# GpSimd takes the negative logits of q from the shifted ones, and the low parts of the MLP weights move behind q's logits on VectorE

## The chip, the cores and the metric

One core of one Trainium2 chip runs the whole kernel as one launch. The metric is the time of the launch in microseconds (us), as the device counts it; the median of repeated runs is given. Smaller is better. The engines are named as the profile names them: PE (TensorE, matrix products), PEld (its weight loads), DVE (VectorE), ACT (ScalarE), POOL (GpSimd) and SP (SyncE, which issues most DMAs).

## What is computed

The input x has 2048 tokens of 512 channels. First comes a linear attention with 32 heads of 16 channels, then an MLP across the tokens, each behind a layer norm and with a residual:

```
q, k, v = split(layernorm(x) @ wqkv)
pq = q @ w_phi (per head);  pk likewise
phi_q = concat(softmax(pq), softmax(-pq));  phi_k likewise
num = phi_q @ (phi_k^T v);  den = phi_q . sum(phi_k) + 1e-6
h  = x + (num / den) @ wo
h2 = h + (gelu(layernorm(layernorm(h))^T @ w1 + b1) @ w2 + b2)^T
```

What matters here is the pair of softmaxes per head of 16 channels: for the first the logits are shifted by their maximum (v - max), for the second the negated logits are shifted by the minimum (min - v). Both halves then go through one exponential.

## The kernel before, in words

**Tiles.** The 2048 tokens are cut into 16 tiles of 128. Every large product is made in three passes from operands that are split into a high and a low part: the high part is a rounded copy made on ACT, the low part is the difference (source minus high part), made on DVE or POOL. `mm3` (L60) issues the three matmuls, so L62, L63 and L64 stand for most of PE's work before the last stage.

**Stages.** (1) The projections of k and v with their softmax and sums, together with the q projections of tiles 0 to 5; (2) a ramp, L420 to L508, that ends k and v, sums k's features over all tiles (`zacc`, finished on DVE in L480 and spread by a product with ones in L487) and starts q's tiles 6 to 9; (3) the loop of L630, one iteration `it` per tile, which makes the attention's output and the residual and fills the first two pairs of MLP columns; (4) the rest of the MLP's first product, then its second product (L761), to the end.

**Order.** From L419 to L669 the order of the instructions on PE, DVE, ACT and POOL is the order of the program text: each engine takes its instructions one after the other, and one that waits holds up all behind it. SP's order, and the order after L669, is set by the planner.

**q's logits.** `logit_ops` (L137) returns three steps for one tile of q, whose projection lies in PSUM (`pu`): the maximum over each head (`mx`, L152), the minimum (`mn`, L153), and `shift`, which writes v - max into the first half of `eq` (L145). For tiles 6 to 15 (`pool` is true), `shift` also has ACT copy the raw logits from PSUM into the second half of `eq` (L147), and `negate` (L156), which is called later, has POOL turn that half into min - v (L160). For other tiles DVE makes both halves (L150). The exponential is L171. The PSUM tile is free for the next product once its last reader is done: DVE's L145 and ACT's L147.

**One iteration of the loop,** for the parts that matter here. PE: `s_num` (L543, the attention's numerator of tile it-1 into the PSUM tile `tn`), `s_wo` (tile it-2 times wo, into `po`), `s_tr` (transposes of tile `it` into `tn`, L525), a q projection (into `pu`), and `fill` products of the MLP (into `pu` too, L62 to L64 with `hs` and `whi`/`wlo`). `tn` has one buffer, so the transposes of a tile wait until ACT's `oh` (L547) and DVE's `ol` (L552) have read the numerator of the tile before. ACT: `pht` (L527), the exponential, the raw copy (L147), `hn` and `hs` (L584, L57), high parts of MLP weights (`whi`, L604), then in the next iteration `oh`. POOL: `s_pq` (L460), `s_rstd` (L579, L580), `s_ez` (L442), `negate` (L160), the low part of `hs` (L58). DVE: the list `ops` of L652, in which the steps of `ol`, of q's logits and of q's sums (L216) take turns with the six steps of `s_den` (L451 to L457); into it go `s_h` (L568, the residual) and `flush` (L593), which makes the low parts of the weights (`wlo`, L596) whose high parts are there.

Iterations 0 to 5 have logits of q in this list; from iteration 6 on there are none left.

Of the kernel before, what the change touches and what calls it, by code (L numbers as in the profile page):

```python
# [11 lines left out]
AF = mybir.ActivationFunctionType  # L12
# [5 lines left out]
P = 128  # L18
S, D, H, DH, F = 2048, 512, 32, 16, 1792
NT = S // P  # L20
# [3 lines left out]
NPR = 2 * NG  # L24
# [9 lines left out]
def block_kernel(ctx: ExitStack, tc: tile.TileContext, x, xT, wT, phic, wo, w1, b1, w2, b2,  # L34
                 kvmask, ident_in, out):
    nc = tc.nc
# [95 lines left out]
    MN = []  # L132

    def signs(e):
        return e.rearrange("p g (a c h d) -> p (g a) c h d", a=2, c=2, h=2)

    def logit_ops(src, e, pool):  # L137

        v = src.rearrange("p (j h d) -> p j h d", h=2, d=DH)
        ev = signs(e)  # L140
        mx = wk.tile([P, NPR, 2], F32, name="mx")
        mn = wk.tile([P, NPR, 2], F32, name="mn")

        def shift():
            nc.vector.tensor_sub(ev[:, :, 0], v, mx.unsqueeze(3).to_broadcast([P, NPR, 2, DH]))  # L145
            if pool:
                nc.scalar.activation(ev[:, :, 1], v, AF.Copy)  # L147
                MN.append((ev, mn))
            else:
                nc.vector.tensor_sub(ev[:, :, 1], mn.unsqueeze(3).to_broadcast([P, NPR, 2, DH]), v)  # L150

        return [lambda: nc.vector.tensor_reduce(mx, v, axis=AX.X, op=ALU.max),  # L152
                lambda: nc.vector.tensor_reduce(mn, v, axis=AX.X, op=ALU.min),  # L153
                shift]

    def negate():  # L156

        if MN:
            ev, mn = MN.pop(0)
            nc.gpsimd.tensor_sub(ev[:, :, 1], mn.unsqueeze(3).to_broadcast([P, NPR, 2, DH]), ev[:, :, 1])  # L160

    def turns(*lists):

        return [ops[i] for i in range(max(map(len, lists))) for ops in lists if i < len(ops)]

    def run(*lists):
        for op in turns(*lists):
            op()
# [42 lines left out]
    def q_sum(t):  # L211

        assert t < SUMS or t - SUMS in W, "a tile's sums would go where others are still wanted"
        SQ[t] = sums[:, t % SUMS]
        e = signs(EQ[t])
        return [lambda c=c: nc.vector.reduce_sum(SQ[t][:, :, 1 - c], e[:, :, c], axis=AX.X) for c in range(2)]  # L216
# [144 lines left out]
    def q_mm():  # L361
        if q["mm"] < NT:
            PS[q["mm"]] = proj(q["mm"], wqh, wql, ps_q, "pu")
            q["mm"] += 1

    def q_logits(lag):
        n = q["logits"]
        if n < min(NT, q["mm"] - lag + NT * (q["mm"] == NT)):
            EQ[n] = big.tile([P, NG, P], F32, name="eq", tag="big")
            q["logits"] += 1  # L370
            return logit_ops(PS[n], EQ[n], n >= len(Q_AT))
        return []
# [7 lines left out]
    def q_sums(lag):  # L380
        n = q["sum"]
        if n < min(NT, q["exp"] - lag + NT * (q["exp"] == NT)):
            q["sum"] += 1
            return q_sum(n)
        return []
# [10 lines left out]
    v = 2  # L396
# [62 lines left out]
    def s_pq(t):  # L459
        nc.gpsimd.tensor_mul(heads(EQ[t]), heads(EQ[t]), W[t].rearrange("p g c h -> p (g c h)").unsqueeze(2).to_broadcast([P, 2 * H, DH]))  # L460

    def lead(it, mm):

        if 0 <= it + 3 < NT:
            s_ez(it + 3)
        negate()
        for _ in range(mm):
            q_mm()
        q_exp(0)
# [51 lines left out]
    def s_tr(t):  # L521
        PHT[t] = ak.tile([P, NG, P], F32, name="pht")
        ptr = ps_t.tile([P, 2, 4, P], F32, name="tn")
        for g in range(NG):
            nc.tensor.transpose(ptr[:, g // 4, g % 4, :], EQ[t][:, g, :], ident)  # L525
        for half in range(2):
            nc.scalar.activation(PHT[t][:, half * 4:half * 4 + 4, :], ptr[:, half], AF.Copy)  # L527

    def s_kv():

        pt = ps_o.tile([P, 2, P], F32, name="po")
        for b in range(2):
            nc.tensor.transpose(pt[:, b, :], kvS[:, 2 * b:2 * b + 2, :].rearrange("p n f -> p (n f)"), ident)
        nc.scalar.activation(kvB, pt, AF.Copy)

    def s_num(t):

        pn = ps_t.tile([P, 2, 4, P], F32, name="tn")[:, :, 0:2]
        for b in range(2):
            for c in range(4):  # L540
                for r in range(2):
                    rows, cols = slice(64 * r, 64 * r + 64), slice(32 * c, 32 * c + 32)
                    nc.tensor.matmul(pn[cols, r, b, :], kvB[rows, b, cols], PHT[t][rows, 4 * b + c, :],  # L543
                                     start=True, stop=True, skip_group_check=True)
        oh = ak.tile([P, 2, 2, P], F32R, name="oh")
        ol = ak.tile([P, 2, 2, P], F32R, name="ol")
        nc.scalar.activation(oh, pn, AF.Copy)  # L547
        OS[t] = oh, ol, pn

    def s_ol(t):  # L550
        oh, ol, pn = OS[t]
        return [lambda: nc.vector.tensor_sub(ol, pn, oh)]  # L552

    def s_wo(t):
        oh, ol, _ = OS.pop(t)
        PO[t] = po = ps_o.tile([P, D], F32, name="po")
        for j in range(4):
            mm3(po, oh[:, j // 2, j % 2, :], ol[:, j // 2, j % 2, :], woh[:, j, :], wol[:, j, :], j == 0, j == 3)

    def s_x(t):  # L560
        HT[t] = ak.tile([P, D], F32, name="h", bufs=4)
        nc.sync.dma_start(HT[t], x[t * P:(t + 1) * P, :])

    def s_h(t):

        h = HT[t]
        VE[t] = ak.tile([P, 4], F32, name="ve2", bufs=3)
        nc.vector.scalar_tensor_tensor(h, PO.pop(t), 1.0, h, op0=ALU.mult, op1=ALU.add, accum_out=VE[t][:, 2:3])  # L568
        nc.sync.dma_start(out[t * P:(t + 1) * P, :], h)

    def s_moments(t):

        junk = ak.tile([P, D], F32, name="hj", bufs=1)
        nc.scalar.activation(VE[t][:, 1:2], VE[t][:, 2:3], AF.Copy, scale=-1.0 / D)
        nc.scalar.activation(junk, HT[t], AF.Square, bias=VE[t][:, 1:2], accum_out=VE[t][:, 3:4])
        nc.scalar.activation(VE[t][:, 0:1], VE[t][:, 3:4], AF.Identity, scale=(1.0 + EPS) / D, bias=eps2)

    def s_rstd(t):
        nc.gpsimd.tensor_tensor(r2[:, t:t + 1], VE[t][:, 0:1], mhalf[:, :1], op=ALU.pow)  # L579
        nc.gpsimd.tensor_mul(VE[t][:, 1:2], VE[t][:, 1:2], r2[:, t:t + 1])  # L580

    def s_hn(t):
        hn = ak.tile([P, D], F32, name="hn")
        nc.scalar.activation(hn, HT[t], AF.Identity, scale=r2[:, t:t + 1], bias=VE[t][:, 1:2])  # L584
        HN[t] = big.tile([P, 2, D], F32R, name="hs", tag="big")
        split(HN[t][:, 0], HN[t][:, 1], hn, nc.gpsimd)
# [29 lines left out]
    def fill(p, pool=None):  # L616

        t = FN[p]
        FN[p] = t + 1
        if FL[p] <= t:  # L620
            fill_load(p)
            flush()
        if t == 0:
            PU[p] = [pool.tile([P, D], F32, name="pu", tag="pu") for _ in range(2)]
        a, b = WI[p, t - t % 2]
        for c in range(2):
            mm3(PU[p][c], a[:, t % 2, c * P:(c + 1) * P], b[:, t % 2, c * P:(c + 1) * P],
                HN[t][:, 0], HN[t][:, 1], t == 0, t == NT - 1)

    for it in range(NT + 3):  # L630
        if 0 <= it < NT:
            s_x(it)
        if 0 <= it - 1 < NT:
            s_num(it - 1)
        if 0 <= it - 3 < NT:
            s_moments(it - 3)
        if 0 <= it - 2 < NT:
            s_wo(it - 2)
        if it == 1:
            run(q_logits(0))  # L640
            q_mm()
        if 0 <= it < NT:
            s_tr(it)
        if it == 0:
            s_kv()
        if 0 <= it + 1 < NT:
            s_pq(it + 1)
        if 0 <= it - 3 < NT:
            s_rstd(it - 3)
        lead(it, 1)  # L650
        den = s_den(it + 2) if it + 2 < NT else []
        ops = turns((s_ol(it - 1) if 0 <= it - 1 < NT else []) + q_logits(1) + (q_sums(0) if it > 0 else []), den)  # L652

        ops[3:3] = ([lambda: s_h(it - 2)] if 0 <= it - 2 < NT else []) + [flush]
        run(ops)
        if it > 0:
            negate()
        if 0 <= it - 3 < NT:
            s_hn(it - 3)
        if FN[0] <= it - LAG:  # L660
            fill(0, ps_f)
        for _ in range(2):
            if q["logits"] == NT and FN[1] <= it - LAG:
                fill(1, ps_q)
        for p in range(2):
            if it >= LAG - 2 and FL[p] <= FN[p] + 1:
                fill_load(p)
# [199 lines left out]
```

## Time and profile before

| What | Value |
|---|---|
| median of 3 runs | 534.8 us (534.78 to 535.04) |
| profiled execution, its own time | 535.27 us |
| its span, first to last instruction | 533.5 us |
| mean granted TensorE clock | 0.999 |
| PE, DVE, ACT, POOL busy | 98%, 72%, 52%, 43% of the span |

The span of the profiled execution is shorter than its time by 1.77 us, which lie before the first and behind the last instruction. PE is busy for nearly all of the span, so what counts is where PE waits: a view of waits lists who waited for whom, and a timeline of one engine gives for each instruction its start, its duration, its line, output and inputs, and in square brackets the idle time before it with what ended it. Matmuls overlap, so that on PE the distance from start to start tells more than the duration.

### The profile page before, as it was taken

The page shows a single profiled execution, that of the slowest core. Times are in us where ns is not written, and L with a number is a line of the kernel's source. Part 1 is how long each engine was busy: PE and PEld are TensorE (multiplying, and loading weights), DVE is VectorE, ACT ScalarE, POOL GpSimd, SP SyncE. Part 2 cuts the span into 40 slices and gives each one's busy share as a digit, 9 for nine tenths or more (in the row PEclk, how much of TensorE's full clock was granted, in tenths as well). Part 3 has the DMA queues.
Part 4 walks back from the last instruction along what each step waited for, and adds up shares of the span by engine and source line. Part 5 has one row for each costly group of instructions (what it writes and reads, how often), then busy time and mean ns, then how long its engine had stood idle before and what let it go on. Part 6 is the DMA issues. An engine that isn't in the chain of part 4 may idle for free.

```text
span 533.5 us, 9887 instructions
## 1 busy us (share of the span) xinstructions
PE 523.4 (98%) x3872; PEld 451.0 (85%) x3872; DVE 382.5 (72%) x680; ACT 277.6 (52%) x470; POOL 228.3 (43%) x180
## 2 busy tenths in 40 slices
PE   8999999999999899999999999999999999999995
PEld 7888888887877777778788888888899999999995
DVE  6893999878798979784235523835768878887784
ACT  6998833525447777666766423525443343343340
POOL 2589699877876978985345000000001101100110
PEclk9999999999999999999999999999999999999999
DMA  8544310022302223333355333533014556535631
GB/s 303 196 124 119 86 35 21 1 62 78 101 1 83 95 81 119 120 109 111 95 159 182 99 100 99 159 111 87 20 41 110 138 149 146 131 120 120 158 78 43
DMA packets 45487, 55.85 MB, mean 105 GB/s; under 512 B 3968, under 2 KB 33024, under 8 KB 45440
## 3 DMA queue, kind: packets, MB, share of 16 engines
q1 hardware_dynamic: 43136, 51.38, 30.3%
q0 software_dynamic: 2016, 3.67, 5.1%
q8 instruction: 30, 0.49, 0.4%
q10 hardware_dynamic: 288, 0.17, 0.1%
q14 instruction: 17, 0.14, 0.1%
HBM read 46.81 MB, written 8.39 MB: 103 GB/s over the span
## 4 chain that ended last, share of the span: by engine, by line
PE 90%; DVE 5%; ACT 3%; issue 1%; POOL 1%; DVEq 0%; ACTq 0%; POOLq 0%
PE py L761 26%; PE pu L62 12%; PE pu L64 12%; PE pu L63 11%; PE po L62 3%; PE pv L63 2%; PE tn L525 2%; PE pv L64 2%; PE pv L62 2%; PE pk_ps L62 2%; PE po L63 2%; PE po L64 2%; PE pk_ps L64 2%; PE pk_ps L63 2%; PE tn L543 2%; PE kvp L207 1%
## 5 line engine op out<-in xcount | busy, mean ns | idle before, releaser
L799 POOL DMA_DIRECT2D out<-ot x14 | 12.5, 1001 | 212.1 <-DVE ot L797 212.1
L761 PE MATMUL py<-uf,whi 128*128 128x256 f32 x560 | 96.2, 283 | 0.0
L62 PE MATMUL pu<-hs,whi 128*128 128x512 f32 x224 | 87.6, 394 | 0.7 <-ACT eq L147 0.7
L57 ACT ACTIVATE whi<-wraw 128x1792 fp32r<-128x1792 f32 x28 | 47.7, 1705 | 77.9 <-PE py L761 62.9
L63 PE MATMUL pu<-hs,whi 128*128 128x512 f32 x224 | 87.2, 389 | 0.0
L64 PE MATMUL pu<-hs,wlo 128*128 128x512 f32 x224 | 87.0, 390 | 0.2 <-DVE wlo L596 0.2
L761 PEld LDWEIGHTS py<-uf,whi 128*128 128x128 f32 x560 | 83.3, 192 | 0.0
L596 DVE TENSOR_TENSOR wlo<-wraw,whi 128x512 fp32r<-128x512 f32 x56 | 46.3, 841 | 45.2 <-ACT whi L604 44.0
L761 PE MATMUL py<-uf,wlo 128*128 128x256 f32 x280 | 69.9, 283 | 0.0
L58 DVE TENSOR_TENSOR wlo<-wraw,whi 128x1792 fp32r<-128x1792 f32 x28 | 56.6, 2023 | 17.8 <-ACT whi L57 17.8
L604 ACT ACTIVATE whi<-wraw 128x512 fp32r<-128x512 f32 x56 | 34.4, 627 | 45.6 <-PE pu L63 41.6
L62 PEld LDWEIGHTS pu<-hs,whi 128*128 128x128 f32 x224 | 42.1, 188 | 9.3 <-ACT eq L147 1.2
L64 PEld LDWEIGHTS pu<-hs,wlo 128*128 128x128 f32 x224 | 42.1, 188 | 9.3 <-DVE wlo L596 0.6
L761 PEld LDWEIGHTS py<-uf,wlo 128*128 128x128 f32 x280 | 49.7, 192 | 0.0
L63 PEld LDWEIGHTS pu<-hs,whi 128*128 128x128 f32 x224 | 42.1, 188 | 8.4
L442 POOL TENSOR_TENSOR ez<-eq,zB 128x1024 f32<-128x1024 f32 x16 | 39.5, 2474 | 0.1
L761 PE MATMUL py<-un,whi 128*128 128x256 f32 x224 | 38.4, 283 | 0.0
L195 POOL TENSOR_TENSOR pk<-pk,sk 128x1024 f32<-128x1024 f32 x16 | 31.1, 1944 | 9.8 <-DVE sk L194 9.0
L460 POOL TENSOR_TENSOR eq<-eq,w 128x1024 f32<-128x1024 f32 x16 | 31.0, 1940 | 5.9 <-DVE w L457 5.9
L527 ACT ACTIVATE pht<-tn 128x512 f32<-128x512 f32 x32 | 17.4, 596 | 30.8 <-PE tn L525 30.8
L761 PEld LDWEIGHTS py<-un,whi 128*128 128x128 f32 x224 | 33.2, 192 | 0.1
L199 POOL TENSOR_TENSOR zacc<-zacc,pk 128x1024 f32<-128x1024 f32 x13 | 31.3, 2406 | 0.6
(165 smaller groups left out, 1192.8 us busy)
## 6 DMA issues: line engine op xcount, KB each, us to landing
wraw<-in_w SPq DMA_DIRECT2D x112, 256.0 KB, 2.9
xraw<-in_xT SPq DMA_DIRECT2D x16, 256.0 KB, 3.1
xh<-in_x SPq DMA_DIRECT2D x16, 256.0 KB, 2.6
h<-in_x SPq DMA_DIRECT2D x16, 256.0 KB, 3.1
out<-h SPq DMA_DIRECT2D x16, 256.0 KB, 2.0
out<-ot POOLq DMA_DIRECT2D x14, 256.0 KB, 4.6
wraw<-in_wT SPq DMA_DIRECT2D x12, 256.0 KB, 5.0
wo<-in_wo SPq DMA_DIRECT2D x4, 256.0 KB, 4.7
```

Of the source, the lines that this page charges most:

```text
L57: nc.scalar.activation(hi, src, AF.Copy)
L58: lo_engine.tensor_sub(lo, src, hi)
L62: nc.tensor.matmul(o, ah, bh, start=first, stop=False)
L63: nc.tensor.matmul(o, ah, bl, start=False, stop=False)
L64: nc.tensor.matmul(o, al, bh, start=False, stop=last)
L195: nc.gpsimd.tensor_mul(heads(PK[t]), heads(PK[t]), sk.unsqueeze(2).to_broadcast([P, 2 * H, DH]))
L199: nc.gpsimd.tensor_add(zacc, zacc, PK[t])
L442: nc.gpsimd.tensor_mul(EZ[t], EQ[t], zB)
L460: nc.gpsimd.tensor_mul(heads(EQ[t]), heads(EQ[t]), W[t].rearrange("p g c h -> p (g c h)").unsqueeze(2).to_broadcast([P, 2 * H, DH]))
L596: LO.append(nc.vector.tensor_sub(wl_, raw, wh_).ins)
L604: nc.scalar.activation(wh_, raw, AF.Copy)
L761: nc.tensor.matmul(o, a[x], b[:, y], start=start and i == 0, stop=stop and i == 2, skip_group_check=True)
```

## The change

For tiles 6 to 15, ACT's raw copy is gone. `negate` on POOL first makes min - max (an operation on 128x32 elements, written over `mn`), then subtracts the shifted logits from it: (min - max) - (v - max) = min - v. The list `MN` carries `mx` too. In the loop, `flush` is no longer put next to `s_h` but at place 7 of the list where there are logits of q, that is behind `shift`; where there are none it stays where it was.

```diff
         def shift():
             nc.vector.tensor_sub(ev[:, :, 0], v, mx.unsqueeze(3).to_broadcast([P, NPR, 2, DH]))
             if pool:
-                nc.scalar.activation(ev[:, :, 1], v, AF.Copy)
-                MN.append((ev, mn))
+                MN.append((ev, mx, mn))
...
         if MN:
-            ev, mn = MN.pop(0)
-            nc.gpsimd.tensor_sub(ev[:, :, 1], mn.unsqueeze(3).to_broadcast([P, NPR, 2, DH]), ev[:, :, 1])
+            ev, mx, mn = MN.pop(0)
+            nc.gpsimd.tensor_sub(mn, mn, mx)
+            nc.gpsimd.tensor_sub(ev[:, :, 1], mn.unsqueeze(3).to_broadcast([P, NPR, 2, DH]), ev[:, :, 0])
...
-        ops = turns((s_ol(it - 1) if 0 <= it - 1 < NT else []) + q_logits(1) + (q_sums(0) if it > 0 else []), den)
-
-        ops[3:3] = ([lambda: s_h(it - 2)] if 0 <= it - 2 < NT else []) + [flush]
+        ql = q_logits(1)
+        ops = turns((s_ol(it - 1) if 0 <= it - 1 < NT else []) + ql + (q_sums(0) if it > 0 else []), den)
+
+        at = 7 if ql else 3
+        ops[at:at] = [flush]
+        ops[3:3] = [lambda: s_h(it - 2)] if 0 <= it - 2 < NT else []
         run(ops)
```

In iterations 2 to 5 DVE's order was `ol`, L451, `mx`, `s_h`, `flush`, L452, `mn`, L454, `shift`, L455, sum, L456, sum, L457. It is now `ol`, L451, `mx`, `s_h`, L452, `mn`, L454, `shift`, `flush`, L455, sum, L456, sum, L457.

## The prediction

> **What bounds the kernel now.** I read the page's busy times first, then the list of what PE waited for, then the timelines of the engines around each of those waits.
>
> ```profile
> span 533.5 us, 9887 instructions
> ...
> PE 523.4 (98%) x3872; PEld 451.0 (85%) x3872; DVE 382.5 (72%) x680; ACT 277.6 (52%) x470; POOL 228.3 (43%) x180
> ```
> ```profile
> PE tn L525 <- POOL hs L58: 1.4, 1, 1.4
> ...
> PE pu L62 <- ACT eq L147: 0.7, 1, 0.7
> PE pk_ps L487 <- DVE zacc L480: 0.5, 1, 0.5
> PE pu L64 <- DVE wlo L596: 0.2, 1, 0.2
> ```
>
> PE is busy for all but 10.1 us. A change on other engines can only win where PE waits, and these are the only waits of PE behind the start-up. Two lie close to what is changed: the transposes of tile 4 (1.4 us) and a fill product that waits for the raw copy itself (0.7 us). The chain that ended last is PE alone from 386.98 to 525.23:
>
> ```profile
> 386.98 138.25 PE py L761 x1152
> ```
>
> So what PE gains or loses before reaches the end in full, as long as no other engine falls behind. Now the two waits, on PE (start, duration):
>
> ```profile
> 165.25 0.39 PE L64 MATMUL po<-woh,ol 128*128 128x512 f32 x1
> 165.48 1.03 PE L525 MATMUL tn<-ident,eq 128*128 128x128 f32 x8
> ...
> 169.18 0.67 PE L543 MATMUL tn<-pht,kvB 64*32 64x128 f32 x32
> ...
> 172.41 0.39 PE L64 MATMUL po<-woh,ol 128*128 128x512 f32 x1
> 174.16 1.06 PE L525 MATMUL tn<-ident,eq 128*128 128x128 f32 x8 [1.37 <-POOL hs L58]
> ...
> 185.43 0.39 PE L64 MATMUL pu<-hs,wlo 128*128 128x512 f32 x1
> 186.55 0.50 PE L62 MATMUL pu<-hs,whi 128*128 128x512 f32 x1 [0.74 <-ACT eq L147]
> ```
>
> Unhindered, the transposes start 0.23 after the last `po` product (165.25 to 165.48). Tile 4's should start at 172.64 and start at 174.16: **1.52 us** lost. The fill product should start at 185.66 and starts at 186.55: **0.89 us**.
>
> What held tile 4? `tn` has one buffer, read by ACT's `oh` and then by DVE's `ol`:
>
> ```profile
> 167.53 1.15 ACT L171 ACTIVATE eq<-eq,r 128x1024 f32<-128x1024 f32 x1
> 170.85 0.60 ACT L147 ACTIVATE eq<-pu 128x512 f32<-128x512 f32 x1 [2.17 <-DVE eq L145]
> 171.34 0.81 ACT L584 ACTIVATE hn<-h,ve,r 128x512 f32<-128x512 f32 x1
> 172.18 0.63 ACT L57 ACTIVATE hs<-hn 128x512 fp32r<-128x512 f32 x1
> 172.72 0.58 ACT L547 ACTIVATE oh<-tn 128x512 fp32r<-128x512 f32 x1
> ```
> ```profile
> 165.97 0.68 DVE L568 SCALAR_TENSOR_TENSOR h<-po,h 128x512 f32<-128x512 f32 x1
> 166.57 2.81 DVE L596 TENSOR_TENSOR wlo<-wraw,whi 128x512 fp32r<-128x512 f32 x2
> 169.41 0.68 DVE L153 TENSOR_REDUCE mn<-pu 128x32 f32<-128x512 f32 x1
> 170.14 0.68 DVE L145 TENSOR_TENSOR eq<-pu,mx 128x512 f32<-128x512 f32 x1
> 172.38 0.22 DVE L457 TENSOR_TENSOR w<-smq,den 128x64 f32<-128x64 f32 x1
> 173.33 0.69 DVE L552 TENSOR_TENSOR ol<-tn,oh 128x512 fp32r<-128x512 f32 x1 [0.73 <-ACT oh L547]
> ```
> ```profile
> 165.06 0.55 POOL L579 TENSOR_TENSOR r<-ve,mhalf 128x1 f32<-128x1 f32 x1
> 165.69 0.19 POOL L580 TENSOR_TENSOR ve<-ve,r 128x1 f32<-128x1 f32 x1
> 165.84 2.39 POOL L442 TENSOR_TENSOR ez<-eq,zB 128x1024 f32<-128x1024 f32 x1
> 171.52 1.07 POOL L160 TENSOR_TENSOR eq<-mn,eq 128x512 f32<-128x512 f32 x1 [3.29 <-ACT eq L147]
> 172.89 1.27 POOL L58 TENSOR_TENSOR hs<-hn,hs 128x512 fp32r<-128x512 f32 x1 [0.30 <-ACT hs L57]
> ```
>
> The numerator was done at 169.85, but ACT sat idle for 2.17 us until 170.85 for DVE's `shift`, made the raw copy, `hn` and `hs`, and reached `oh` at 172.72. `ol` ended at 174.02, and PE went on at 174.16. (The list names POOL's `hs`, which ended at the same moment. The transposes read neither `hs` nor `hn`, so I take `ol`.) DVE was late because its two `wlo` took 2.81 us, ahead of `mn` and `shift`.
>
> **The port.** Why 2.81? A `wlo` alone took 0.69:
>
> ```profile
> 183.75 0.69 DVE L596 TENSOR_TENSOR wlo<-wraw,whi 128x512 fp32r<-128x512 f32 x1
> ```
>
> POOL's `ez` ended at 168.23; two uncovered operations at the pitch of 0.6 then end at 169.4, which is when the two did (166.57 + 2.81 = 169.38). So the first stood still until `ez` was through. The ramp shows who goes next when both wait:
>
> ```profile
> 125.05 1.29 DVE L480 TENSOR_TENSOR zacc<-zacc,pk 128x512 f32<-128x512 f32 x2 [0.41 <-POOL pk L195]
> ...
> 127.47 1.55 DVE L431 TENSOR_TENSOR wol<-wo,woh 128x512 fp32r<-128x512 f32 x1
> ```
> ```profile
> 123.08 1.94 POOL L195 TENSOR_TENSOR pk<-pk,sk 128x1024 f32<-128x1024 f32 x1 [1.09 <-DVE sk L194]
> 127.07 1.40 POOL L160 TENSOR_TENSOR eq<-mn,eq 128x512 f32<-128x512 f32 x1 [2.05 <-ACT eq L147]
> ```
>
> POOL's `negate` took 1.40 instead of its usual 1.06 (it waited some 0.34 for DVE's running `wol`) and ended at 128.47; the `wol` issued at 127.47 ended at 129.02, 0.55 after it. So they take turns, one instruction each, and the loser waits for the whole one. The operations that collide have both inputs in SBUF (`wlo`, `wol`, `zacc`; all of POOL's here).
>
> **The change part by part.**
>
> ```profile
> L147 ACT ACTIVATE eq<-pu x10: 577/598/601, 126.4 to 185.9; 128x512 f32<-128x512 f32 x10
> L160 POOL TENSOR_TENSOR eq<-mn,eq x10: 1060/1064/1402, 127.1 to 186.8; 128x512 f32<-128x512 f32 x10
> ```
>
> *Removed:* ten ACT copies of 0.598, 6.0 us of ACT. As PE is the bound, only their place counts: ACT no longer waits there for `shift`, and a `pu` buffer is free after `shift`. *Added:* ten POOL operations of 128x32. The trace has none of that size. Bounds: 0.19 (L580, 128x1) and 1.06 (128x512); on the line between them 32 columns give 0.19 + 0.87 x 31/511 = 0.25, and I take that, as it lies near the 128x1 row. The big subtraction needs its result; L580 needs that of L579 and started 0.08 behind it (165.61 to 165.69), so 0.33 for each tile and 3.3 us on POOL in all. It is hidden in the loop: what a `negate` makes is wanted by the exponential of the next iteration, which follows that iteration's transposes as 167.53 follows 165.48, so at 176.2, and iteration 3's `negate` ended at 172.59. If that cover were gone, 0.33 an iteration would show, 2 us at most. The big subtraction keeps its size and 1.06.
>
> *Tile 4's wait, iteration 3.* ACT: exponential to 168.68, `hn` to 169.45, `hs` to 170.05, `oh` to 170.65. DVE: after `s_h` (to 166.57) come L452, `mn`, L454 and `shift` at the same distances as before, so `shift` starts at 170.14 - 2.74 = 167.40 and is issued through at 168.0. First `wlo`: waits for `ez`, 168.23 to 168.8. POOL's small one takes its turn, to 169.05; second `wlo` to 169.65; then the big one. The rest of the list (from 170.73, the end of `shift`'s pitch, to 172.60 before, 1.87) ends at 171.5. `ol` 171.5 to 172.2, `tn` free at 172.3, before 172.64: the wait is gone, **-1.52**. Should POOL run both of its operations between the two `wlo`, or before them, all is 1.1 later and 0.75 us of the wait stay.
>
> *The fill's wait, iteration 5.* `shift` stood behind one `wlo` of pitch 0.6 and then came the copy, which ended at 186.50. Now `shift` ends at about 185.27 without the `wlo`, against 185.66 when PE wants the buffer: **-0.89**, and 0.11 more, as the second product after that wait came 0.34 later instead of 0.23. Hidden by 0.4. Since both parts of this iteration follow PE's numerator, being 1.52 earlier changes nothing in it.
>
> *The new collision, in the ramp.* In the program text `negate` of tile 6 stands directly behind POOL's `pk` of L195, which ends at 125.02. It used to wait for the raw copy until 127.07. Now nothing holds it: `mn` and `shift` of tile 6 were made by 124.64.
>
> ```profile
> 123.96 0.68 DVE L145 TENSOR_TENSOR eq<-pu,mx 128x512 f32<-128x512 f32 x1
> ```
>
> At 125.05 DVE wants its two `zacc` sums, and PE waits for them:
>
> ```profile
> 125.89 1.95 PE L487 MATMUL pk_ps<-zacc,ones 128*128 128x512 f32 x4 [0.45 <-DVE zacc L480]
> ```
> ```profile
> L487 PE MATMUL pk_ps<-zacc,ones x4: 592/592/667, 125.9 to 127.3; 128*128 128x512 f32 x4
> ```
>
> By turns: small POOL operation to 125.25, first `zacc` to 125.8, big one to 126.86, second `zacc` to 127.4 (before: 126.34). The first PE product is 0.05 to 0.1 later. The third, first of the second half, stood at 126.80 (four products, the last of 0.59, end 1.95 after the first starts: 0.45 apart), and now waits for 127.4 + 0.15 (the 0.15 that PE took before, from the first sum's end at 125.74 to 125.89) = 127.55: **+0.75**. Bounds: 0 if DVE gets both of its turns first, 1.2 if POOL does (`zacc` from 126.4, ending at 126.95, PE at 127.1 instead of 125.89).
>
> The Trainium skill, page "SBUF — State Buffer", section "Who interferes with whom", states that a VectorE instruction with two SBUF inputs contends with a GpSimd instruction that reads SBUF, and that the first to issue holds the pair for the whole instruction; by it the sum has this +0.75, and without the rule it would be -2.52. The trace agrees so far: 1.40 us for a `negate` of 1.06 behind a running `wol`.
>
> *Sum:* -1.52 - 1.00 + 0.75 = **-1.77 us**. The wait for `wlo` at L64 (0.2) is in iteration 6, whose list is as before, and stays. The span goes from 533.5 to 531.7, the profiled execution from 535.27 to 533.5; it lies 0.47 above the median of 534.8, so by the same difference the median goes to **533.0 us**.
>
> **The rivals.**
>
> *A, no collision in the ramp.* DVE gets both `zacc` sums through. The only hint for it is that DVE's instruction is already queued; against it, POOL is the first to be ready. Then -2.52: 532.3.
>
> *B, tile 4's wait stays in part or whole.* Either POOL's two operations come between the `wlo` (0.75 stays: -1.02, 533.8), or the list is right that POOL's `hs` releases the transposes and it comes late (1.52 stays: -0.25, 534.55). Against the second: `hs` would be made earlier too, as ACT makes its input 2 us earlier.
>
> *C, slower: POOL wins each turn.* If a ready POOL operation always goes before DVE's, the ramp costs 1.2; in iteration 3 the second `wlo` waits for the small one, the big one and the low part of `hs` (ACT's part ends at 170.05, so to 171.4 at L58's 1.27), DVE ends at 173.8 instead of 172.6 and `ol` at 174.5, so the wait of tile 4 grows to 2.0 (+0.5); in iteration 5 the one `wlo`, now behind `shift`, meets the same row of POOL operations, and if that costs what it adds in iteration 3, it is +0.5 again; the fill's wait is gone (-1.0). Together +1.2: 536.0. It decides at the point where POOL has its next instruction ready when one ends. Against it: in the ramp `wol` got its turn between `negate` and the `ez` behind it.
>
> *D, nothing moves,* because the planned order behind the loop changes, and gives back about 1.8. PE has no wait there now; the profile can't show the planner's choice. 534.8.
>
> **How the numbers follow.** Forecast 0.47 (532.6 to 533.6, from its +0.4 to +1.2 of collision); A 0.14; B 0.18, most of it in 533.6 to 534.6; C 0.13; D 0.08. The range is to hold the forecast, A and B with most of D: 532.1 to 534.9. A difference of 0.2%, 1.07 us, is about what a measurement of this kernel can tell from no change. Faster than 533.73: forecast, A and a third of B, 0.67. Slower than 535.87: C and a little of D, 0.14. Between: 0.19.
>
> **What would show it.** Right: no ACT work at L147; the wait at L525 and that at L62 gone from PE's list; the wait at L487 grown or a second one there, with a `zacc` of about 1.6 us instead of 0.69; `negate` starting at 125.0; `wlo` behind `shift`. Wrong: a PE wait at L525 that is still over 0.5 us (B); a `zacc` pair of 1.3 us (A); `wlo` durations above 3 us and waits at tiles 4 and 6 (C); new PE waits after 262 us (D).

## The result and the profile after

The changed kernel takes 532.88 us (median of 6 runs, 532.59 to 533.53), the kernel before 535.0 us (6 runs, 534.78 to 535.26); the ratio is 0.9963, with a 95% interval of 0.995 to 0.9976, so about 2 us less (2.1 by the medians). The forecast was 533.0 us and 1.8 us less.

The list of what PE waited for, in the changed kernel:

```profile
PE pk_ps L487 <- DVE zacc L480: 0.9, 2, 0.5
...
PE pu L64 <- DVE wlo L596: 0.2, 1, 0.2
```

These are all behind the start-up. The waits at L525 and L62 are gone; at L487 there are two waits of together 0.9 us where there was one of 0.5. That is the forecast's list.

The spans of the two profiled executions, 533.5 and 531.0, differ by 2.5 us, which is more than the medians do. The rest is from the first microseconds, before anything that was changed. On PE, the first projection and the transposes of the last tile, before and then after:

```profile
10.60 0.73 PE L124 MATMUL pk_ps<-wkh,xs 128*128 128x512 f32 x2 [0.80 <-ACT wkh L280]
...
257.26 1.03 PE L525 MATMUL tn<-ident,eq 128*128 128x128 f32 x8
```
```profile
10.02 1.20 PE L124 MATMUL pk_ps<-wkh,xs 128*128 128x512 f32 x4 [0.69 <-ACT wkh L280]
...
254.73 1.03 PE L525 MATMUL tn<-ident,eq 128*128 128x128 f32 x8
```

From the one to the other it is 246.66 us before and 244.71 after: **1.95 us less**. From the last tile's transposes to the end of the span it is 276.24 before (533.5 - 257.26) and 276.27 after (531.0 - 254.73). So what the change does happens between these two points, and nothing is given back behind them. The first projection starts 0.58 us apart: in the profile before, DVE waited 0.74 us for a weight's transfer in the start-up, and in the one after it didn't (the row is in the last section). In the twelve profiles of this document it starts anywhere from 9.88 to 10.81. In what follows "the middle" is this stretch, from the first L124 to the transposes of tile 15; it leaves out the start-up's scatter. How well one profile gives it can be seen from its first part, up to the first product of L487, which takes 115.28 to 115.37 us in all twelve.

**Tile 4's transposes and the fill.** On PE after the change, with the transposes of tiles 3, 4, 5 and 6:

```profile
165.55 1.03 PE L525 MATMUL tn<-ident,eq 128*128 128x128 f32 x8
...
172.71 1.03 PE L525 MATMUL tn<-ident,eq 128*128 128x128 f32 x8
...
181.22 1.03 PE L525 MATMUL tn<-ident,eq 128*128 128x128 f32 x8
...
189.74 1.03 PE L525 MATMUL tn<-ident,eq 128*128 128x128 f32 x8
```

Tile 3 to tile 4 takes 7.16 us instead of 8.68, which is 1.52 less. Tiles 5 and 6 in the kernel before:

```profile
182.72 1.03 PE L525 MATMUL tn<-ident,eq 128*128 128x128 f32 x8
...
192.28 1.03 PE L525 MATMUL tn<-ident,eq 128*128 128x128 f32 x8
```

From tile 4 to 5 it was 8.56 and is 8.51 now; from tile 5 to 6, where the fill waited, it was 9.56 and is 8.52, which is 1.04 less.

Iteration 3 on ACT, DVE and POOL after the change:

```profile
167.60 1.15 ACT L171 ACTIVATE eq<-eq,r 128x1024 f32<-128x1024 f32 x1
168.64 0.81 ACT L584 ACTIVATE hn<-h,ve,r 128x512 f32<-128x512 f32 x1
...
170.03 0.60 ACT L547 ACTIVATE oh<-tn 128x512 fp32r<-128x512 f32 x1
```
```profile
167.27 0.69 DVE L145 TENSOR_TENSOR eq<-pu,mx 128x512 f32<-128x512 f32 x1
167.87 1.34 DVE L596 TENSOR_TENSOR wlo<-wraw,whi 128x512 fp32r<-128x512 f32 x2
...
170.93 0.68 DVE L552 TENSOR_TENSOR ol<-tn,oh 128x512 fp32r<-128x512 f32 x1
```
```profile
165.59 2.38 POOL L442 TENSOR_TENSOR ez<-eq,zB 128x1024 f32<-128x1024 f32 x1
167.92 0.74 POOL L159 TENSOR_TENSOR mn<-mn,mx 128x32 f32<-128x32 f32 x1
168.74 1.39 POOL L160 TENSOR_TENSOR eq<-mn,eq 128x512 f32<-128x512 f32 x1
```

ACT goes from the exponential straight to `hn`, `hs` and `oh`. The two `wlo` take 1.34 us instead of 2.81, as `ez` ends at 167.97, only 0.1 after the first is issued. Then the turns can be read: POOL's small operation, issued at 167.92, takes 0.74 instead of 0.25, and ends just after the first `wlo` does; the big one takes 1.39 instead of 1.06, and the second `wlo` runs ahead of it. `ol` runs at 170.93, a microsecond before PE has need of `tn`.

**The ramp.** DVE, POOL and PE where `zacc` is finished:

```profile
124.52 2.19 DVE L480 TENSOR_TENSOR zacc<-zacc,pk 128x512 f32<-128x512 f32 x2 [0.41 <-POOL pk L195]
```
```profile
122.55 1.94 POOL L195 TENSOR_TENSOR pk<-pk,sk 128x1024 f32<-128x1024 f32 x1 [1.09 <-DVE sk L194]
124.44 0.25 POOL L159 TENSOR_TENSOR mn<-mn,mx 128x32 f32<-128x32 f32 x1
124.77 1.38 POOL L160 TENSOR_TENSOR eq<-mn,eq 128x512 f32<-128x512 f32 x1
```
```profile
125.39 1.10 PE L487 MATMUL pk_ps<-zacc,ones 128*128 128x512 f32 x2 [0.50 <-DVE zacc L480]
126.85 1.10 PE L487 MATMUL pk_ps<-zacc,ones 128*128 128x512 f32 x2 [0.36 <-DVE zacc L480]
```

POOL starts on tile 6 while its `pk` is only just through, 0.08 us ahead of DVE's first sum. The pair of sums takes 2.19 us instead of 1.29, and the third product stands 1.46 us behind the first instead of 0.91: 0.55 us lost, where 0.75 was forecast.

### The profile page after: what moved, and what is told of

Same layout as the page of the kernel before. It is cut to its first block, busy times and chain, and to the rows that moved or that the text cites. A ratio compares the mean times of both kernels' runs of the same rounds, so it can differ in the third digit from the quotient of the medians.

```text
span 531.0 us, 9886 instructions
## 1 busy us (share of the span) xinstructions
PE 522.6 (98%) x3872; PEld 450.6 (85%) x3872; DVE 379.0 (71%) x680; ACT 272.2 (51%) x460; POOL 231.0 (44%) x190
## 4 chain that ended last, share of the span: by engine, by line
PE 93%; DVE 4%; ACT 1%; issue 1%; POOL 0%; DVEq 0%; ACTq 0%; POOLq 0%
PE py L764 26%; PE pu L62 12%; PE pu L64 12%; PE pu L63 12%; PE po L62 3%; PE po L63 3%; PE po L64 3%; PE tn L525 3%; PE pv L63 2%; PE pv L64 2%; PE pv L62 2%; PE pk_ps L62 2%; PE pk_ps L64 2%; PE pk_ps L63 2%; PE tn L543 2%; PE kvp L207 1%
## 5 line engine op out<-in xcount | busy, mean ns | idle before, releaser
L62 PE MATMUL pu<-hs,whi 128*128 128x512 f32 x224 | 87.6, 394 | 0.0
L64 PE MATMUL pu<-hs,wlo 128*128 128x512 f32 x224 | 87.1, 390 | 0.2 <-DVE wlo L596 0.2
L596 DVE TENSOR_TENSOR wlo<-wraw,whi 128x512 fp32r<-128x512 f32 x56 | 45.1, 816 | 48.2 <-ACT whi L604 47.8
L58 DVE TENSOR_TENSOR wlo<-wraw,whi 128x1792 fp32r<-128x1792 f32 x28 | 56.6, 2023 | 18.1 <-ACT whi L57 18.0
L64 PEld LDWEIGHTS pu<-hs,wlo 128*128 128x128 f32 x224 | 42.1, 188 | 9.3 <-DVE wlo L596 0.6
L62 PEld LDWEIGHTS pu<-hs,whi 128*128 128x128 f32 x224 | 42.1, 188 | 8.4
```

What stands on the lines that cost most here:

```text
L58: lo_engine.tensor_sub(lo, src, hi)
L62: nc.tensor.matmul(o, ah, bh, start=first, stop=False)
L64: nc.tensor.matmul(o, al, bh, start=False, stop=last)
L596: LO.append(nc.vector.tensor_sub(wl_, raw, wh_).ins)
```

## Experiments

The theory on trial is that the move of `flush` takes tile 4's wait away and helps the fill, and that the removal of the copy brings a collision of POOL and DVE in the ramp. The prediction had taken the two edits together; e1 and e2 take them one by one. The rivals are that the copy alone held both waits, that the collision is none, that the transposes wait for POOL's `hs`, and that POOL goes first whenever it is ready. e1 to e4 and e8 to e10 have 5 to 11 runs each, and each of their medians stands beside that of the kernel before in the same series; the middle is that of one profile. "The port" is short for what DVE and POOL take turns at: while an operation of the one runs there, a colliding one of the other stands still. (The middle: 246.66 us before, 244.71 after the change.)

| Kernel | Median, us | Before, us | Ratio (95% interval) | Middle, us |
|---|---|---|---|---|
| e1: copy gone, flush not moved | 534.6 | 534.83 | 0.9993 (0.9984 to 1.0001) | 246.78 |
| e2: flush moved, copy kept | 533.35 | 534.83 | 0.9968 (0.9957 to 0.9979) | 244.99 |
| e3: the change, tile 6 later on POOL | 532.33 | 534.83 | 0.9952 (0.994 to 0.9965) | 244.10 |
| e4: the change, tile 6 keeps the copy | 532.05 | 534.83 | 0.9947 (0.9934 to 0.9961) | 244.04 |
| e8: e4, flush first in iteration 6 | 532.19 | 535.14 | 0.9952 (0.9939 to 0.9966) | 244.01 |
| e9: e8, flush last from iteration 7 on | 531.91 | 535.12 | 0.9938 (0.9925 to 0.9952) | 243.42 |
| e10: e1, flush last from iteration 7 on | 533.99 | 535.12 | 0.9983 (0.9974 to 0.9992) | 245.76 |

### e1: the copy alone

```diff
...
-        ops[at:at] = [flush]
-        ops[3:3] = [lambda: s_h(it - 2)] if 0 <= it - 2 < NT else []
+        ops[3:3] = ([lambda: s_h(it - 2)] if 0 <= it - 2 < NT else []) + [flush]
```

> Half of the change: the raw copy is gone, flush stays at its old place next to s_h. Theory (the move of flush is the larger half, and the copy's removal brings a collision in the ramp): DVE is still late by its two wlo in iteration 3, so of the wait of tile 4's transposes about 0.75 of 1.5 us stays; of the fill's wait 0.1 to 0.2 stays; the third L487 product is 0.6 later. Together about -1.1 us against before. Rival (the copy on ACT was what held both waits, and the moved flush adds nothing): both waits gone, about -2.1 us, as with the whole change.

The median is 0.2 us below before, with an interval that includes no change, and the middle is 0.12 longer: neither number was met. (The profiled execution took 535.36 us, the longest of e1's eleven, which begin at 533.92.) What PE waited for, in e1:

```profile
PE tn L525 <- DVE ol L552: 0.9, 1, 0.9
PE pk_ps L487 <- DVE zacc L480: 0.9, 2, 0.5
...
PE pu L64 <- DVE wlo L596: 0.6, 1, 0.6
PE tn L525 <- POOL hs L58: 0.2, 1, 0.2
```

The ramp has its second wait, as expected. At tile 4 less is left than expected: 0.2 us of idle time (the list again names `hs`, which ended at nearly the same moment as `ol`), and 7.53 us from tile 3 to tile 4, 0.37 more than in the changed kernel. So the copy's removal alone takes 1.15 of the 1.52 us. DVE's two `wlo` are as slow as before, and `ol` comes at the end of DVE's list:

```profile
172.74 0.68 DVE L552 TENSOR_TENSOR ol<-tn,oh 128x512 fp32r<-128x512 f32 x1
```

It no longer waits for ACT, as it did for 0.73 us before. The fill's wait at L62 is below what the list shows (0.18 us from start to start); from tile 5 to 6 it is 8.85 us, so 0.71 of the 1.04 us is won and 0.33 left. But there is a new wait of 0.9 us at L525 that nobody had expected, far behind the edits, at the transposes of tile 10. On PE, DVE and POOL of e1:

```profile
221.49 1.06 PE L525 MATMUL tn<-ident,eq 128*128 128x128 f32 x8 [0.89 <-DVE ol L552]
```
```profile
214.17 4.58 DVE L596 TENSOR_TENSOR wlo<-wraw,whi 128x512 fp32r<-128x512 f32 x2
...
220.66 0.68 DVE L552 TENSOR_TENSOR ol<-tn,oh 128x512 fp32r<-128x512 f32 x1
```
```profile
214.11 2.41 POOL L442 TENSOR_TENSOR ez<-eq,zB 128x1024 f32<-128x1024 f32 x1
216.88 1.32 POOL L58 TENSOR_TENSOR hs<-hn,hs 128x512 fp32r<-128x512 f32 x1 [0.36 <-ACT hs L57]
```

`ez` was issued 0.06 us ahead of the first `wlo`. So that one stood behind all of `ez`, and the second behind `hs`: 4.58 us for two operations of 0.6. In the kernel before, the same place went the other way:

```profile
215.22 1.29 DVE L596 TENSOR_TENSOR wlo<-wraw,whi 128x512 fp32r<-128x512 f32 x2
```
```profile
215.91 2.85 POOL L442 TENSOR_TENSOR ez<-eq,zB 128x1024 f32<-128x1024 f32 x1
```

DVE came first, POOL's `ez` took 2.85 us instead of 2.4, and PE had no wait. What e1 gained at tile 4 and at the fill (1.9 us in all) it gave back in the ramp (0.55), at tile 10 (1.0) and at L64 (0.4; its idle time is 0.55 instead of 0.17 us). e10 tests this.

The same rows tell who releases the transposes. `hs` had ended at 218.20, 3.3 us before they start; `ol` ended at 221.34, 0.15 before. At tile 4 in the kernel before it was 0.14 from the end of `ol` (174.02 to 174.16).

### e2: the move of flush alone

```diff
             if pool:
-                MN.append((ev, mx, mn))
+                nc.scalar.activation(ev[:, :, 1], v, AF.Copy)
+                MN.append((ev, mn))
...
```

(This is against the changed kernel. `negate` too is as it was before; the list `ops` is the changed one.)

> The other half: flush goes behind shift, the raw copy stays. Theory: shift comes early enough that ACT's copy, hn, hs and oh and then ol are done before 172.6, so the wait of tile 4's transposes is gone (-1.5); the fill still waits about 0.3 us for the copy (-0.7); no collision in the ramp, one wait of 0.5 at L487 as before. Together about -2.2 us, no less than the whole change. Rival (the copy's removal is what counts): the copy still stands before hn, hs and oh, so most of the wait stays and the time is within 0.7 us of before.

The median is 1.5 us below before and the middle 1.67 shorter. Tile 4's wait is gone and the ramp has its one wait of 0.5, as expected. The fill still waits, for longer than expected. PE and ACT in e2:

```profile
184.62 0.50 PE L62 MATMUL pu<-hs,whi 128*128 128x512 f32 x1 [0.64 <-ACT eq L147]
```
```profile
182.93 1.15 ACT L171 ACTIVATE eq<-eq,r 128x1024 f32<-128x1024 f32 x1
183.97 0.60 ACT L147 ACTIVATE eq<-pu 128x512 f32<-128x512 f32 x1
```

Here it is not `shift` that the copy waits for, but ACT itself: the exponential ends at 184.08, and the copy stands behind it. It was so in the kernel before too, where the copy started at 185.90:

```profile
184.77 1.15 ACT L171 ACTIVATE eq<-eq,r 128x1024 f32<-128x1024 f32 x1
```

So an earlier `shift` hardly helps while the copy is there: from tile 5 to 6 it is 9.48 us instead of 9.56. The rival as it was put falls: with the copy kept, tile 4's wait is gone. But the copy was no bystander there. Either edit alone takes most of that wait (1.15 us without the copy, all 1.52 with `flush` moved), so it can't be credited to one of them.

### e3 and e4: without the collision

e3 puts POOL's two operations for tile 6 behind the first `ez`; e4 lets tile 6 alone keep the copy, so that POOL waits for it as before.

```diff
     for j in range(KD):
         wo_lo(j)
-    negate()
...
-    q_exp(0)
     s_ez(0)
+    negate()
+    q_exp(0)
     s_ez(1)
```

> The whole change, but POOL's two operations for tile 6 come behind the first ez instead of right behind pk, so that nothing of POOL runs when DVE makes the zacc sums. Theory (a collision of POOL and DVE in the ramp): the zacc pair takes 1.3 us again instead of 2.2, the second wait at L487 is gone, and PE is 0.6 us earlier from there on; about -2.7 us against before, -0.6 against the changed kernel. Rival (the wait at L487 grew because PE itself arrived 0.5 us earlier in that execution): the second wait stays, and the time is that of the changed kernel, -2.1.

```diff
-            if pool:
+            if pool and raw:
+                nc.scalar.activation(ev[:, :, 1], v, AF.Copy)
+                MN.append((ev, None, mn))
+            elif pool:
                 MN.append((ev, mx, mn))
...
+            if mx is None:
+                nc.gpsimd.tensor_sub(ev[:, :, 1], mn.unsqueeze(3).to_broadcast([P, NPR, 2, DH]), ev[:, :, 1])
+                return
...
-            return logit_ops(PS[n], EQ[n], n >= len(Q_AT))
+            return logit_ops(PS[n], EQ[n], n >= len(Q_AT), n == len(Q_AT))
```

> The whole change for tiles 7 to 15; tile 6 keeps the raw copy on ACT, so that POOL's subtraction for it waits for ACT until about 127 us. Theory (collision): as with POOL's operations put later, zacc pair 1.3 us, one wait at L487, about -2.7 us against before. Rival (no collision): -2.1, as with the whole change.

Both came as the theory had it: 2.5 and 2.8 us below before by the median, and a middle that is 2.56 and 2.62 shorter, so 0.61 and 0.67 shorter than with the whole change. DVE's sums in e3:

```profile
124.74 1.29 DVE L480 TENSOR_TENSOR zacc<-zacc,pk 128x512 f32<-128x512 f32 x2 [0.41 <-POOL pk L195]
```

The pair takes 1.29 us again. The rival, that the second wait at L487 came from PE's earlier arrival, falls too: e3's first projection is early (10.23) and it has one wait, e1's is as late as that of before (10.52) and it has two.

### e5, e6, e7: what holds whom

Each of these is one execution, and is read from its trace.

e5 makes POOL's low part of `hs` of tile 0 three times, so that POOL is late but DVE's `ol` isn't.

```diff
         split(HN[t][:, 0], HN[t][:, 1], hn, nc.gpsimd)
+        for _ in range(2 if t == 0 else 0):
+            nc.gpsimd.tensor_sub(HN[t][:, 1], hn, HN[t][:, 0])
```

> The changed kernel, with POOL's low part of hs for tile 0 made three times (same result), so that POOL's work there ends about 2.5 us later, at some 174 in the changed kernel's profile. Theory (the transposes of tile 4 wait for DVE's ol, as tn has one buffer): they still start 7.16 us after those of tile 3, without a wait. Rival (they wait for POOL's hs, as the list of waits has it): they start 8.4 us or more after, with a wait of over 1 us at L525.

POOL's and PE's rows in e5, the latter of tiles 3, 4 and 5:

```profile
172.38 2.66 POOL L588 TENSOR_TENSOR hs<-hn,hs 128x512 fp32r<-128x512 f32 x2
...
181.37 1.29 POOL L58 TENSOR_TENSOR hs<-hn,hs 128x512 fp32r<-128x512 f32 x1
```
```profile
166.37 1.03 PE L525 MATMUL tn<-ident,eq 128*128 128x128 f32 x8
...
173.52 1.03 PE L525 MATMUL tn<-ident,eq 128*128 128x128 f32 x8
...
182.03 1.03 PE L525 MATMUL tn<-ident,eq 128*128 128x128 f32 x8
```

POOL is done at 175.04, and tile 4's transposes start at 173.52, 7.15 us behind tile 3's and without a wait. That alone is not quite enough: only the two added operations are late there, and the first `hs` ended at 172.31, ahead of the transposes. Tile 5 settles it. POOL is late as a whole by then, and the transposes start at 182.03 while `hs` of the iteration before (L58, as it always was) runs until 182.66. So they don't need `hs`, and the name in the list of before was a coincidence of two ends. (e5 has a wait of 0.8 us at tile 8, where two `wlo` took 3.49 us beside POOL: 533.99 us.)

e6 makes POOL's big subtraction of tile 6 twice.

```diff
-    negate()
+    negate(1)
...
+    def negate(again=0):
...
+            for _ in range(1 + again):
+                nc.gpsimd.tensor_sub(ev[:, :, 1], mn.unsqueeze(3).to_broadcast([P, NPR, 2, DH]), ev[:, :, 0])
```

> The changed kernel, with POOL's big subtraction of tile 6 made twice (same result). Theory (POOL and DVE take turns, one instruction each): DVE's second zacc sum waits for one of them only, the zacc pair takes 2.2 us and the third L487 product starts 1.46 us after the first, as in the changed kernel; the second subtraction delays wol. Rival (POOL goes first whenever it is ready): the pair takes 3.2 us or more and the third product starts 2.5 us after the first.

DVE and POOL in e6:

```profile
124.45 2.19 DVE L481 TENSOR_TENSOR zacc<-zacc,pk 128x512 f32<-128x512 f32 x2 [0.41 <-POOL pk L196]
```
```profile
124.70 2.85 POOL L161 TENSOR_TENSOR eq<-mn,eq 128x512 f32<-128x512 f32 x2
```

The sums still take 2.19 us: between POOL's two subtractions DVE got its turn. The third product at L487 is 1.46 us behind the first, as before. POOL has no priority; this rules out the slower rival of the prediction. The second subtraction only makes `wol` late, which PE doesn't wait for (532.7 us).

e7 puts work that only writes in the place of tile 6's operations.

```diff
+    nc.gpsimd.memset(pad[:, 0:32], 0.0)
+    nc.gpsimd.memset(pad, 0.0)
```

(On top of e3; `pad` is a tile that nothing reads.)

> POOL's operations of tile 6 come late, behind the first ez; in their old place, right behind pk, POOL fills a tile that nothing reads with zeros, once 32 and once 504 columns, so it writes SBUF and reads nothing. Theory (the collision is over reading SBUF, and needs two readers): the zacc pair takes 1.3 us, one wait at L487. Rival (any work of POOL on SBUF holds DVE's two-input operations up): the pair takes over 1.6 us and a second wait at L487 is there.

```profile
124.51 0.13 POOL L483 MEMSET pad<- 128x32 f32 x1
124.69 0.52 POOL L484 MEMSET pad<- 128x504 f32 x1
```
```profile
124.61 1.29 DVE L480 TENSOR_TENSOR zacc<-zacc,pk 128x512 f32<-128x512 f32 x2 [0.41 <-POOL pk L195]
```

Both fills lie beside the sums, and the sums are not held up: 1.29 us, one wait at L487 (532.22 us). So writing alone does not hold the sums up; POOL's operations that collide all read. That DVE has to have two inputs in SBUF fits the rows that the prediction shows (`s_h`, with one of its inputs in PSUM, took its usual 0.68 beside `ez`), but no run tries it by itself. The Trainium skill, page "SBUF — State Buffer", section "Who interferes with whom", says that a GpSimd instruction that only writes SBUF does not contend with such a VectorE instruction, and this run agrees with it.

### e8, e9, e10: who is first at the port, and a faster kernel

e8 goes after the last wait in the loop, at L64 in iteration 6, where `wlo` stands behind `ez`: there `flush` comes first in DVE's list.

```diff
-        at = 7 if ql else 3
+        at = 7 if ql else 0 if it == 6 else 3
         ops[at:at] = [flush]
-        ops[3:3] = [lambda: s_h(it - 2)] if 0 <= it - 2 < NT else []
+        ops[3 + (it == 6):3 + (it == 6)] = [lambda: s_h(it - 2)] if 0 <= it - 2 < NT else []
```

(On top of e4.)

> The kernel in which tile 6 keeps the raw copy, and in iteration 6 flush comes first in DVE's list, where DVE waits for oh anyway. Theory: the last wait of PE in the loop (0.2 us at L64, in all 0.4 us) goes, since wlo is done before ez starts; 0.4 us below that kernel, about -3.1 us against before. Rival (wlo meets POOL's hs there and makes ol late): a wait at L525 in its place, no gain.

The wait at L64 is gone, but the median is that of e4 (532.19 to 532.05), and the middle too (244.01 to 244.04). In its place, in e8:

```profile
PE tn L531 <- DVE ol L558: 0.4, 1, 0.4
```
```profile
197.95 3.08 DVE L602 TENSOR_TENSOR wlo<-wraw,whi 128x512 fp32r<-128x512 f32 x2
```

One iteration later the two `wlo` meet `ez`, and all of DVE's list stands behind them, down to the `ol` that tile 8's transposes wait for. e4 has much the same there, 3.06 us; but with PE 0.5 us earlier (7.15 us from tile 6 to 7 instead of 7.67) it now shows. What was gained was taken at the next narrow place.

e9 takes that place away too: from iteration 7 on, when `wlo` isn't wanted before the next iteration, `flush` is the last entry of the list.

```diff
-        at = 7 if ql else 0 if it == 6 else 3
+        at = 7 if ql else 0 if it == 6 else len(ops)
```

(On top of e8.)

> As the kernel with tile 6's raw copy and flush first in iteration 6, and from iteration 7 on flush is the last entry of DVE's list, behind the weights' last step L463, instead of behind s_h. Theory (in iteration 7 ez takes the port ahead of the two wlo, and DVE's whole list stands behind them, ol with it): the wait of 0.4 us at L531 goes and none takes its place, about 0.5 us below that kernel, 531.7 us, -3.3 against before. Rival (each wait that is removed in the loop comes back in a later iteration): another wait of 0.3 to 1 us at L531 or L64, no gain.

PE has no wait left between L493 (L487 of the kernels without the lines of e4) and the end. Behind the start-up the list of e9 has that one wait:

```profile
PE pk_ps L493 <- DVE zacc L486: 0.4, 1, 0.4
```

The middle is 243.42, 3.24 us below before and 1.29 below the changed kernel; the median is 531.91, ratio 0.9938. This kernel beats the one before in the same series, and its five runs (531.75 to 532.28) lie below the six of the changed kernel (532.59 to 533.53), which were taken in another series. The rival falls.

e10 gives e1 the same late `flush`, to see whether tile 10's wait was its loss.

```diff
-        ops[3:3] = ([lambda: s_h(it - 2)] if 0 <= it - 2 < NT else []) + [flush]
+        ops[3:3] = ([lambda: s_h(it - 2)] if 0 <= it - 2 < NT else []) + ([flush] if it < 7 else [])
+        ops += [flush] if it >= 7 else []
```

(On top of e1.)

> The kernel with the raw copy gone and flush at its old place, but from iteration 7 on flush is the last entry of DVE's list. Theory (that kernel lost 1.1 us at tile 10's transposes, because ez took the port 0.06 us ahead of DVE and its two wlo took 4.6 us): that wait is gone, about -1.2 us against before instead of -0.2. Rival (it lost its gain elsewhere): -0.2 as it was.

1.1 us below before by the median, and a middle of 245.76, 1.02 below e1's. Tile 10's wait is gone; the ramp's second wait, 0.2 at tile 4 and 0.6 at L64 stay. So of what e1 gave back, 1.0 us was lost to a race at the port. It is the rows that show this; by the times alone the intervals of e1 and e10 overlap, and as only one of e1's executions has a trace, it is not known whether each of them lost that race.

## Why the prediction was right

By its steps, with the middle of the two profiles (1.95 us less; the sum was 1.77):

- **Tile 4's wait, -1.52:** measured -1.52 (8.68 to 7.16 us from tile to tile). The releaser is DVE's `ol`, as argued: e5 rules out `hs`, and e1's tile 10 starts 0.15 us behind `ol`. The forecast named both edits together and did not split them. The move of `flush` alone takes all of it (e2), the copy's removal alone 1.15 us (e1): they overlap.
- **The fill's wait, -1.00:** measured -1.04. The prediction put it down to both edits, `shift` without the `wlo` ahead of it and no copy behind it. The copy's removal alone gives 0.71 us (e1), the move of `flush` alone 0.08 (e2), as the copy stood behind ACT's exponential too. The remaining 0.25 us comes only with both. In the kernel before, the end of `shift` (185.87) and that of the exponential (185.92) lay side by side, and the prediction had read the first alone.
- **The collision in the ramp, +0.75:** measured +0.55 at L487 and +0.61 and +0.67 by e3 and e4. The term that was too large is the end of the big subtraction: 1.81 us after the issue of the first sum was worked out (126.86 - 125.05), and the rows have 1.63 (124.77 + 1.38 - 124.52). The first sum was hardly held up by the small operation (the first product's idle time is 0.50 us instead of 0.45).
- **The sum:** the three terms as measured add up to -2.01 us, 0.06 from the middle's 1.95. Single profiles do not tell so little apart.
- **The small operation:** 0.25 us was taken (the line between the two rows gives 0.24), 0.25 measured where nothing holds it, and over 0.7 in two of the ten, where a `wlo` was running; 0.08 to the next one, 0.08 measured (124.69 to 124.77).
- **The rivals.** A (no collision) falls by e3 and e4. B (a rest of tile 4's wait, or `hs`) falls by the trace and by e5. C (POOL wins each turn) falls by e6. D (something is given back behind the loop) falls by the stretch from the last tile's transposes to the end, 276.2 to 276.3 us in all twelve profiles.

What the prediction did not have is that the order of two issues at the port, 0.06 us apart, can cost 1.0 us, half of what the change is worth (e1 and e10). In the changed kernel the places in iterations 7 to 15 fell well, with no wait of PE; the sum took that as given, without a step for it. So the number was right partly by the luck of these places, and e1 shows what the other outcome costs.

## What to carry to other kernels

An operation that waits for less runs earlier, and what it then meets is part of the price: look for the work of the other engine that it slips next to, above all where GpSimd reads SBUF while VectorE has two inputs there and PE waits for the result. When two edits aim at the same wait, run each alone: here either would have taken most of it. When a wait in a list names an engine, compare the end of every other reader of the buffer; two ends 0.1 us apart can be told apart by making one of them late, if it is the very instruction in question that comes late. Small work that isn't wanted soon goes behind the operations that release PE, not ahead of them.

## What the runs showed of the hardware

- The scatter of the start: the first projection began between 9.88 and 10.81 us in the twelve profiles, of kernels that are the same up to there. In the profile before, DVE stood idle for 0.74 us until a weight had landed, and after the change it didn't. Differences of the span below a microsecond should be read behind that point.

```profile
5.88 0.69 DVE L256 TENSOR_REDUCE mu<-wraw 128x1 f32<-128x512 f32 x1 [0.74 <-DMA wraw<-in_wT]
```

- A race at the port: two `wlo` took 1.29 us where DVE was first and 4.58 where POOL's `ez` was issued 0.06 us ahead of them and `hs` came in between.
- Turns: two subtractions of POOL in a row left DVE's two sums at 2.19 us, the same as one did (e6).
- A GpSimd operation that only writes SBUF (0.52 us for 504 columns) ran beside VectorE's sums and cost them nothing.
